# Fused windowed attention and squared-ReLU MLP: dense steps, products, transposes and an overlap copy put in another order

## The chip, the cores and the metric

The kernel runs on one core of a Trainium2 chip. The metric is the device time of one execution in microseconds. The kernel before took 306.08 us, the median of five runs (305.75 to 309.16).

## The reference

Attention over 8 batch rows, 8 heads, 576 positions and 64 values a head, then a two-layer MLP. Heads 0 to 3 see the last 32 positions (sliding), heads 4 to 7 every fourth of the last 128 (dilated).

```python
def _attn_ref(q, k, v):
    B, H, S, D = q.shape                       # 8, 8, 576, 64
    scores = 1.0 / np.sqrt(D) * np.matmul(q, k.transpose(0, 1, 3, 2))
    rel = pos[:, None] - pos[None, :]
    mask_plain = (rel >= 0) & (rel < 32)
    mask_dil = (rel >= 0) & (rel < 128) & (rel % 4 == 0)
    ...
    attn = np.exp(scores - max)
    attn = attn / (np.sum(attn, axis=-1, keepdims=True) + 1e-09)
    return np.matmul(attn, v)

def _moe_ref(x, w_in, w_out):                  # x 4608x512, w_in 512x2048, w_out 2048x512
    h = x @ w_in
    r = np.maximum(h, 0.0)
    return (r * r) @ w_out
```

## The kernel before

**Two kinds of work on TensorE.** A *row* is one of the 8 batch rows of attention (576 tokens). A *dense group* c is 512 of the 4608 tokens in the MLP, so there are 9, numbered 0 to 8. Row b's attention runs interleaved with dense group b − 1. Dense work is written as Python generators in the list `pending`; `pump(n)` (L521) takes n steps of it. So the order of every engine's instructions is written out by hand: attention code issues some matmuls, calls `pump(gap)`, issues the next. `manual_schedule` (L70) keeps that order; each engine executes its own instructions in the order written and waits on semaphores for operands and free buffers. A PSUM tile comes from `papool` (tag pa, 2 buffers, attention) or `pmool` (tag pm, 4 buffers, dense work and some transposes).

**A dense group.** `mm1_gen` (L319) makes 16 tiles ph of 128×512 (L305), with two matmuls a step and four a tile; ScalarE applies ReLU (rt, L328) and VectorE squares it (g, L329). After tiles 11 and 15, `sum_of_g` (L336) makes sums of g, gs[0] and gs[1] (L338, L339). Groups 0 and 1 multiply by w_out plainly (po, L450; group 0 in the order of `mm2_by_rows_gen`). Groups 2 to 8 use `mm2_strassen_gen` (L360): seven products of 256-wide matmuls (L382) into three PSUM banks A, Bk and Ck, shown by the profile as pa, pb and pc. Each product is 2 token tiles × 8 matmuls, and a step ends after four of them. `take` (L396) has ScalarE copy bank A out (ou for the upper half, ov for the lower), `add` (L408) has VectorE add another bank, `leave` (L401) stores on SP's DMA queue. VectorE overwrites gs[1] once in the course of it (L425), since a later product takes other sums.

**A row.** `attn_scores` (L713) makes two groups of sliding scores (ps, L588) and two of dilated ones (pz, L613), each followed by exponentials on ScalarE (L572), masks on VectorE (L575) and a `pump`. `attn_values` (rows 1 to 3) and `attn_values_by_dma` (rows 4 to 7) multiply by v (sliding: pav, L643, three tiles; dilated: paw, L659, four), with a reciprocal and a scaling by VectorE each (L626, L631 into xs and xd), and bring x into xT.

**What a row needs beforehand.** Transposed q and k come from DMA: GpSimd's queue loads ns (sliding) and rewrites the dilated q and k in DRAM as dd; VectorE reorders ns into nr (`by_token`, L120); SP's queue writes nr to DRAM as dp (L224) and transposes dp into QKTp (L232) and dd into QKTd (L236). `turn` (L859) is reorder and dp together. Row 1 alone has its transposes on TensorE (pt L545, pd L562). v is loaded by SP as f32 into sv and sd (L132, L137), and GpSimd casts it into vp and vd (L169, L177). Blocks of v overlap: the last 32 partitions of vp's block m − 1 are needed also as the first 32 of block m, and 64 partitions of vd likewise. Rows 0 to 2 copy the overlap on ScalarE (L184, L189); row 3 and row 4 by SP's DMA (L201, L204); rows 5 to 7 copy that of vp on VectorE (L196) at the end of the dense group and that of vd by DMA (L204).

**Where the loads of rows 3 and 4 stand.** `turn_and_load` (L874) issues on SP: dp, sv, sd, then the transposes QKTp and QKTd, and on GpSimd both casts. For row 3 it is called in row 2's `attn_values` after the third pav; for row 4 as a hook of row 3's `attn_scores` after the last dilated scores. At the top of the next iteration GpSimd waits for the row's transposes (`after_transposes`, L241, a copy into `seen`) and then issues ns and dd of the row after. Rows 5 to 7 already have their transposes ahead of sd and cast vd after the ns and dd issues.

Of the kernel before, what the change touches and what calls it, by code (L numbers as in the profile page):

```python
# [13 lines left out]
P = 128  # L14
# [3 lines left out]
def kernel(  # L18
# [9 lines left out]
    nc = tc.nc  # L28
# [18 lines left out]
    NB = S // QB  # L47
    PADP = P - QB
# [33 lines left out]
    HF = NFF // 2  # L82
    HTOK = TOKC // 2
    wt = [wpool.tile([P, HF, HM], FP16, name=f"wt{n}") for n in range(4)]
    gs = [wpool.tile([P, HF, HTOK], FP16, name=f"gs{n}") for n in range(2)]
# [48 lines left out]
    def load_dilated_v(b, eng):  # L134
        vv = v[b, HH:H].rearrange("h (i c) d -> i h (c d)", c=DIL)
        for t in range(2):
            eng.dma_start(out=sd[P - QD[t] : P, t, :, :], in_=vv[Q0D[t] : Q0D[t] + QD[t]])  # L137
# [54 lines left out]

    at_end: list = []

    def halo_sliding_at_end(b):
        nc.vector.tensor_copy(  # L196
            vp[b % 2][0:PADP, 1:NB, :, 0:D], vp[b % 2][P - PADP : P, 0 : NB - 1, :, 0:D]
        )

    def halo_sliding_by_dma(b):  # L200
        nc.sync.dma_start(out=vp[b % 2][0:PADP, 1:NB], in_=vp[b % 2][P - PADP : P, 0 : NB - 1])  # L201

    def halo_dilated_by_dma(b):
        nc.sync.dma_start(out=vd[b % 2][0:64, 1], in_=vd[b % 2][64:P, 0])  # L204
# [1 line left out]
    def cast_v(b):  # L206
        cast_sliding_v(b)
        cast_dilated_v(b)
# [75 lines left out]
    for r in range(2):  # L284
        nc.vector.tensor_scalar(
            out=vd[r][:, 0, :, :, D],
# [73 lines left out]
    def mm2_strassen_gen(c, g):  # L360
        A, Bk, Ck = "abc"
        banks = {}

        def wq(r, q):
            return lambda k: wo[2 * r + k // 4][:, k % 4, HM * q : HM * (q + 1)]

        def gq(i, r):
            return lambda k, t: g[:, HF * r + k, HTOK * i + P * t : HTOK * i + P * (t + 1)]

        def tq(n):  # L370
            return lambda k: wt[n][:, k]

        def sq(n):
            return lambda k, t: gs[n][:, k, P * t : P * (t + 1)]

        def product(bank, a, b, ts=(0, 1)):
            new = bank not in banks
            if new:
                banks[bank] = pmool.tile([P, 2, HM], FP32, name=f"p{bank}{c}", tag="pm")
            for t in ts:  # L380
                for k in range(HF):
                    nc.tensor.matmul(  # L382
                        banks[bank][:, t],
                        a(k, t),
                        b(k),
                        start=(new and t == 0 and k == 0),
                        stop=(k == HF - 1),
                        skip_group_check=True,
                    )
                    if k % 4 == 3 and (t, k) != (ts[-1], HF - 1):  # L390
                        yield

        def half(i):
            return otp.tile([P, 2, DM], FP32, name=f"o{i}_{c}", tag="ot")

        def take(o, j):  # L396
            ot = o[:, :, HM * j : HM * (j + 1)]
            nc.scalar.copy(ot, banks[A])  # L398
            return ot

        def leave(o, i, js):  # L401
            t0 = c * TOKC + HTOK * i
            m = slice(HM * js[0], HM * (js[-1] + 1))
            nc.sync.dma_start(
                out=out[t0 : t0 + HTOK, m].rearrange("(t p) m -> p t m", p=P), in_=o[:, :, m]
            )

        def add(ot, bank):  # L408
            nc.vector.tensor_add(ot, banks[bank], ot)  # L409

        last = c == NTOKC - 1

        nc.vector.tensor_sub(g[:, 0:HF, HTOK:], g[:, 0:HF, 0:HTOK], g[:, 0:HF, HTOK:])
        yield from product(A, gq(0, 0), wq(0, 0))
        upper = half("u")
        o11 = take(upper, 0)
        yield
        yield from product(Ck, gq(0, 1), wq(1, 0), (0,))
        yield
        yield from product(A, sq(1), tq(1))  # L420
        lower = half("v")
        o21 = take(lower, 0)
        yield
        yield from product(Bk, gq(1, 0), tq(2))
        nc.vector.tensor_sub(gs[1], g[:, HF:, 0:HTOK], gs[1])  # L425
        yield
        yield from product(A, sq(0), tq(0))
        o22 = take(lower, 1)
        add(o22, Bk)
        if last:  # L430
            leave(lower, 1, (1,))
        yield
        yield from product(Ck, gq(0, 1), wq(1, 0), (1,))
        add(o11, Ck)
        if last:
            leave(upper, 0, (0,))
        yield
        yield from product(A, sq(1), wq(1, 1))
        take(upper, 1)
        leave(upper, 0, (1,) if last else (0, 1))  # L440
        while at_end:
            at_end.pop()()
        yield
        yield from product(Bk, gq(1, 1), tq(3))
        add(o21, Bk)
        leave(lower, 1, (0,) if last else (0, 1))
        yield
# [73 lines left out]
    def pump(n):  # L521
        for _ in range(n):
            while pending:
                try:
                    next(pending[0])
                    break
                except StopIteration:
                    pending.pop(0)
# [184 lines left out]
    def attn_scores(b, gap, less=0, hooks={}):  # L713
        for hp in range(2):
            s_sliding(b, hp)
            if hp in hooks:
                hooks[hp]()
            pump(gap)
        for g in range(2):
            s_dilated(b, g)  # L720
            if 2 + g in hooks:
                hooks[2 + g]()
            if g and b < 3:
                halo_sliding(b, 0)
            pump(gap - less)

    def attn_values(b, gap, wide=False, then=None):
        xs = x_tiles(b)
        for mp in range(3):
            av_sliding(b, mp, xs)  # L730
            if b < 3:
                if mp < 2:
                    halo_sliding(b, mp + 1)
                else:
                    halo_dilated(b, 0)
            if then and b == 2 and mp == 2:
                then()
            pump(gap)
        x_sliding(b, 0, xs, wide)
        if b < 3:  # L740
            halo_dilated(b, 2)
        pump(gap)
        av_dilated(b, 0, 0, xs)
        if then and b == 1:
            then()
        pump(gap)
        x_sliding(b, 1, xs, wide)
        pump(gap)
        av_dilated(b, 0, 1, xs)
        pump(gap)  # L750
        for a in range(2):
            av_dilated(b, 1, a, xs)
            pump(gap)
        x_dilated(b, 0, xs, wide)
        pump(gap)
        x_dilated(b, 1, xs, wide)
# [85 lines left out]
    n, m = nsd[1]  # L842
    for hp in range(2):
        t_sliding(1, n, hp, True)
        pump(3)
    for a in range(2):
        t_dilated(1, m, a, True)
        pump(2)
    attn_scores(1, 2, 1)
    dp = []  # L850
    attn_values(1, 1, True, lambda: dp.append(keep_sliding_qk(2, by_token(2, ns))))
    pump(1000)
# [9 lines left out]
    for b in range(2, 4):  # L862
        pending.append(moe_gen(b - 1))
        nxt = b + 1
        after_transposes(b)
        ns = load_sliding_qk(nxt)
        if b == 2:
            cast_v(b)
        dd = keep_dilated_qk(nxt)
        if b == 3:  # L870
            halo_sliding_by_dma(b)
            halo_dilated_by_dma(b)

        def turn_and_load():  # L874
            dp = turn(nxt, ns)
            load_sliding_v(nxt)
            load_dilated_v(nxt, nc.sync)
            transpose_sliding(nxt, dp)
            transpose_dilated(nxt, dd)
            cast_v(nxt)  # L880

        pump(22 if b == 2 else 12)
        attn_scores(b, 4, 0, {3: turn_and_load} if b == 3 else {})
        attn_values(b, b, False, turn_and_load)
        pump(1000)

    for b in range(4, B):
        pending.append(moe_gen(b - 1))
        nxt = b + 1
        if nxt < B:  # L890
            after_transposes(b)
            ns = load_sliding_qk(nxt)
            dd = keep_dilated_qk(nxt)
        if b > 4:
            cast_dilated_v(b)
        else:
            halo_sliding_by_dma(b)
        halo_dilated_by_dma(b)
        dps = []

        def copied():
            if nxt < B:
                dps.append(turn(nxt, ns))

        def first(y):
            if nxt < B:
                load_sliding_v(nxt)

        def second(y):
            if nxt < B:  # L910
                transpose_sliding(nxt, dps[0])
                transpose_dilated(nxt, dd)
                load_dilated_v(nxt, nc.sync)
                nc.gpsimd.tensor_copy(seen, y[:, 0, 0, 0:1])
                cast_sliding_v(nxt)
                at_end.append(lambda: halo_sliding_at_end(nxt))

        pump(3)
        attn_scores(b, 3)
        attn_values_by_dma(b, (copied, first, second))  # L920
        pump(1000)
# [33 lines left out]
```

## Time and profile before

| | |
|---|---|
| median of five runs | 306.08 us |
| the profiled execution's own time | 305.86 us |
| its span in the trace | 304.1 us |
| PE busy | 287.3 us |
| VectorE (DVE) busy | 211.0 us |
| ScalarE (ACT) busy | 173.3 us |
| GpSimd (POOL) busy | 63.3 us |
| DMA packets' time, share of 16 engines, SP's queue / GpSimd's | 51.1% / 26.5% |

The span is the time from the first to the last instruction in the trace; 1.8 us of the execution's own time lie around it. Row 1's transposes and attention lie between 40 and 62 us, row 3's from 100.6 to about 127, rows 4, 5, 6 and 7 begin at 128.4, 158.2, 188.9 and 219. Groups 7 and 8 run alone from 248 us on; PE ends at 300. In a timeline row stand the start, the duration, the engine, the line, out<-in and the count, and at the end in brackets the engine's idle time before it with the releaser. In a row of the table of stretches stand the stretch, its length, the engine's busy time (and count), the granted clock, the DMA share and GB/s. Matmul ends are modelled, so starts are the better measure.

### The profile page before, as it was taken

The page shows a single profiled execution, that of the slowest core. Times are in us where ns is not written, and L with a number is a line of the kernel's source. Part 1 is how long each engine was busy: PE and PEld are TensorE (multiplying, and loading weights), DVE is VectorE, ACT ScalarE, POOL GpSimd, SP SyncE. Part 2 cuts the span into 40 slices and gives each one's busy share as a digit, 9 for nine tenths or more (in the row PEclk, how much of TensorE's full clock was granted, in tenths as well). Part 3 has the DMA queues.
Part 4 walks back from the last instruction along what each step waited for, and adds up shares of the span by engine and source line. Part 5 has one row for each costly group of instructions (what it writes and reads, how often), then busy time and mean ns, then how long its engine had stood idle before and what let it go on. Part 6 is the DMA issues. An engine that isn't in the chain of part 4 may idle for free.

```text
span 304.1 us, 6890 instructions
## 1 busy us (share of the span) xinstructions
PE 287.3 (94%) x2760; PEld 192.6 (63%) x2760; DVE 211.0 (69%) x437; ACT 173.3 (57%) x293; POOL 63.3 (21%) x112
## 2 busy tenths in 40 slices
PE   1888998999999999999999999999999999999994
PEld 1555554455554458755898977557756975785583
DVE  7684548858862798589849994999399834734652
ACT  2765648578835863495359544953496346425620
POOL 4491009001613502320027002700230000000000
PEclk9999999999999999999999999999999999999999
DMA  7899996999689999996799999998983230003004
GB/s 114 192 186 215 207 183 110 178 220 232 127 193 188 249 190 200 229 215 125 132 158 267 192 139 189 267 175 161 173 243 30 49 136 4 2 1 138 2 1 138
DMA packets 77471, 46.77 MB, mean 154 GB/s; under 512 B 58432, under 2 KB 69184, under 8 KB 77440
## 3 DMA queue, kind: packets, MB, share of 16 engines
q1 hardware_dynamic: 68688, 32.71, 51.1%
q0 software_dynamic: 8752, 13.63, 26.5%
q8 instruction: 21, 0.34, 0.5%
q14 instruction: 10, 0.08, 0.1%
HBM read 36.70 MB, written 16.52 MB: 175 GB/s over the span
## 4 chain that ended last, share of the span: by engine, by line
PE 74%; DMA 10%; DVE 9%; POOL 2%; issue 2%; ACT 1%; SPq 0%; DVEq 0%; POOLq 0%
PE ph L305 30%; PE pa L382 15%; PE po L450 8%; PE pb L382 8%; DMA vd<-vd 4%; PE pc L382 3%; DMA nd<-in_q_dram 3%; PE paw L659 2%; DVE g L329 2%; DVE AT L575 2%; DMA QKTp<-dp 2%; DVE xd L631 2%; PE pf L516 2%; DMA QKTd<-dd 1%; PE pav L643 1%
## 5 line engine op out<-in xcount | busy, mean ns | idle before, releaser
L305 PE MATMUL ph<-xT,wi 128*128 128x512 f16 (+1 forms) x640 | 134.2, 359 | 0.7 <-ACT xT L696 0.7
L328 ACT ACTIVATE rt<-ph 128x512 f16<-128x512 f32 x144 | 86.2, 609 | 44.9 <-PE ph L305 42.5
L305 PEld LDWEIGHTS <-wi 128*128 128x128 f16 x640 | 68.2, 114 | 45.8 <-issue 0.6
L329 DVE TENSOR_TENSOR g<-rt 128x512 f16<-128x512 f16 x144 | 62.4, 445 | 37.9 <-ACT rt L328 36.8
L382 PEld LDWEIGHTS <-g 128*128 128x128 f16 x448 | 43.3, 98 | 6.5 <-DVE g L329 0.4
L382 PEld LDWEIGHTS <-gs 128*128 128x128 f16 x336 | 32.0, 98 | 5.4 <-DVE gs L339 1.8
L450 PE MATMUL po<-wo,g 128*128 128x512 f16 x128 | 33.1, 379 | 0.0
L382 PE MATMUL pa<-wt,gs 128*128 128x256 f16 x224 | 27.6, 273 | 1.0 <-DVE gs L339 1.0
L409 DVE TENSOR_TENSOR ov<-pb,ov 128x512 f32<-128x512 f32 x14 | 9.7, 691 | 25.7 <-ACT ov L398 13.0
L382 PE MATMUL pb<-wt,g 128*128 128x256 f16 x224 | 27.1, 273 | 0.0
L398 ACT COPY ov<-pa 128x512 f32<-128x512 f32 x14 | 8.2, 585 | 31.4 <-PE pa L382 31.4
L169 POOL CAST vp<-sv 128x512 f16<-128x512 f32 x24 | 14.8, 646 | 52.4 <-DMA sv<-in_v_dram 41.6
L177 POOL CAST vd<-sd 128x512 f16<-128x512 f32 (+1 forms) x32 | 21.7, 708 | 10.2 <-DMA sd<-in_v_dram 7.9
L631 DVE TENSOR_TENSOR xd<-paw,rcp_d 80x512 f16<-80x512 f32 (+1 forms) x32 | 21.9, 685 | 1.1
L572 ACT ACTIVATE AT<-pz 128x576 f16<-128x576 f32 x32 | 19.8, 695 | 1.2 <-PE pz L613 1.1
L575 DVE TENSOR_TENSOR AT<-AT,maskd 128x576 f16<-128x576 f16 x32 | 18.7, 611 | 1.7 <-ACT AT L572 0.6
L572 ACT ACTIVATE AT<-ps 128x576 f16<-128x576 f32 x32 | 19.2, 658 | 1.3 <-PE ps L588 0.8
L575 DVE TENSOR_TENSOR AT<-AT,maskp 128x576 f16<-128x576 f16 x32 | 15.9, 510 | 4.9 <-ACT AT L572 3.4
L631 DVE TENSOR_TENSOR xs<-pav,rcp_p 96x512 f16<-96x512 f32 x24 | 16.5, 687 | 0.8
L398 ACT COPY ou<-pa 128x512 f32<-128x512 f32 x14 | 8.2, 585 | 13.4 <-PE pa L382 13.4
L450 PEld LDWEIGHTS <-g 128*128 128x128 f16 x128 | 10.4, 97 | 8.3
L659 PEld LDWEIGHTS <-AT 128*128 128x128 f16 x256 | 11.9, 98 | 5.6 <-PE paw L659 1.3
(81 smaller groups left out, 276.3 us busy)
## 6 DMA issues: line engine op xcount, KB each, us to landing
sv<-in_v_dram SPq DMA_DIRECT2D x14, 288.0 KB, 5.2
dp<-nr SPq DMA_DIRECT2D x12, 288.0 KB, 3.9
out_dram<-ou SPq DMA_DIRECT2D x6, 512.0 KB, 4.2
out_dram<-ov SPq DMA_DIRECT2D x6, 512.0 KB, 4.4
sd<-in_v_dram SPq DMA_DIRECT2D x8, 320.0 KB, 5.7
ns<-in_k_dram POOLq DMA_DIRECT2D x8, 288.0 KB, 6.8
ns<-in_q_dram POOLq DMA_DIRECT2D x8, 288.0 KB, 8.0
sd<-in_v_dram SPq DMA_DIRECT2D x8, 256.0 KB, 5.2
```

The source lines that it names most:

```text
L169: nc.gpsimd.tensor_copy(vp[b % 2][:, m : m + 2, :, 0:D], sv[:, :, m : m + 2, :].rearrange("p h m d -> p m h d"))
L177: nc.gpsimd.tensor_copy(vd[b % 2][p0:P, t, c : c + 2, :, 0:D], sd[p0:P, t, :, D * c : D * (c + 2)].rearrange("p h (c d) -> p c h d", d=D),)
L305: nc.tensor.matmul(ph[:, t0:t1], wi4[ffc // 4][:, dmk, :, ffc % 4], xT[:, dmk, x0 : x0 + t1 - t0], start=(dmk == 0 and t0 == 0), stop=(dmk ...
L328: nc.scalar.activation(rt, ph[:], ACTF.Relu)
L329: nc.vector.tensor_mul(g[:, ffc, :], rt, rt)
L382: nc.tensor.matmul(banks[bank][:, t], a(k, t), b(k), start=(new and t == 0 and k == 0), stop=(k == HF - 1), skip_group_check=True,)
L398: nc.scalar.copy(ot, banks[A])
L450: nc.tensor.matmul(po, g[:, ffc, t * P : (t + 1) * P], wo[ffc // 4][:, ffc % 4, :], start=(ffc == 0), stop=(ffc == NFF - 1),)
L572: nc.scalar.activation(AT[:, u, 0:UW], ps[:, :, 0 : UW // 2], ACTF.Exp, scale=scale)
L575: nc.vector.tensor_mul(AT[:, u, 0:UW], AT[:, u, 0:UW], mask)
L631: nc.vector.tensor_tensor(out=x, in0=pv, in1=rb, op=ALU.mult)
L659: nc.tensor.matmul(pav[:, e, h * (D + 2) : h * (D + 2) + D + 1], AT[:, 4 + h, off : off + P], vd[b % 2][:, t, 2 * a + e, h, 0 : D + 1], st ...
```

## The change

- `mm2_strassen_gen` (all groups from 2 on): the product of Ck runs whole after the first product of A, with the add of o11 right behind it, where it had stood in two halves. The second half of Bk's product takes the place of the second half of Ck's. The gs[1] subtraction stands after `take` instead of behind Bk's product.
- Row 1: `pump(3)` after each sliding transpose becomes 2, that after the second dilated transpose 1; the pumps after the two dilated score groups become 2 instead of 1, the one after pav 0 becomes 2. The sum stays 17 steps.
- Rows 3 and 4: transposes go ahead of sd on SP's queue. For row 4 the whole of it (nr, dp, sv, transposes, sd) moves from the hook after row 3's last scores to after row 3's second pav. GpSimd casts only vp there; vd is cast after the ns and dd issues of the next iteration. The overlap of vp is copied by VectorE: for row 3 as a hook after the second sliding scores, for row 4 at the end of dense group 2; the two DMAs go.
- Row 3's first pump is 9 steps instead of 12, so three more dense steps stand behind the scores.

On the engines, built: SP loses two vp DMAs, ScalarE's and PE's instruction counts stay, VectorE has two copies more. On SP the last stores of the closing group change places (the first half of u ahead of the second half of v).

```diff
-    def halo_sliding_at_end(b):
+    def halo_sliding_at_once(b):
         nc.vector.tensor_copy(
             vp[b % 2][0:PADP, 1:NB, :, 0:D], vp[b % 2][P - PADP : P, 0 : NB - 1, :, 0:D]
         )
-
-    def halo_sliding_by_dma(b):
-        nc.sync.dma_start(out=vp[b % 2][0:PADP, 1:NB], in_=vp[b % 2][P - PADP : P, 0 : NB - 1])
@@ mm2_strassen_gen
-        yield from product(Ck, gq(0, 1), wq(1, 0), (0,))
+        yield from product(Ck, gq(0, 1), wq(1, 0))
+        add(o11, Ck)
+        if last:
+            leave(upper, 0, (0,))
         yield
         yield from product(A, sq(1), tq(1))
         lower = half("v")
         o21 = take(lower, 0)
+        nc.vector.tensor_sub(gs[1], g[:, HF:, 0:HTOK], gs[1])
         yield
-        yield from product(Bk, gq(1, 0), tq(2))
-        nc.vector.tensor_sub(gs[1], g[:, HF:, 0:HTOK], gs[1])
+        yield from product(Bk, gq(1, 0), tq(2), (0,))
         yield
         yield from product(A, sq(0), tq(0))
         o22 = take(lower, 1)
+        yield
+        yield from product(Bk, gq(1, 0), tq(2), (1,))
         add(o22, Bk)
         if last:
             leave(lower, 1, (1,))
-        yield
-        yield from product(Ck, gq(0, 1), wq(1, 0), (1,))
-        add(o11, Ck)
-        if last:
-            leave(upper, 0, (0,))
         yield
         yield from product(A, sq(1), wq(1, 1))
@@ attn_values
-            if then and b == 2 and mp == 2:
+            if then and b > 1 and mp == 4 - b:
                 then()
-            pump(gap)
+            pump(gap + (b == 1 and mp == 0))
@@ row 1
         t_sliding(1, n, hp, True)
-        pump(3)
+        pump(2)
     for a in range(2):
         t_dilated(1, m, a, True)
-        pump(2)
-    attn_scores(1, 2, 1)
+        pump(2 - a)
+    attn_scores(1, 2)
@@ rows 2 and 3
         if b == 3:
-            halo_sliding_by_dma(b)
+            cast_dilated_v(b)
             halo_dilated_by_dma(b)
 
         def turn_and_load():
             dp = turn(nxt, ns)
             load_sliding_v(nxt)
-            load_dilated_v(nxt, nc.sync)
             transpose_sliding(nxt, dp)
             transpose_dilated(nxt, dd)
-            cast_v(nxt)
-
-        pump(22 if b == 2 else 12)
-        attn_scores(b, 4, 0, {3: turn_and_load} if b == 3 else {})
+            load_dilated_v(nxt, nc.sync)
+            cast_sliding_v(nxt)
+            if nxt > 3:
+                at_end.append(lambda: halo_sliding_at_once(nxt))
+
+        pump(22 if b == 2 else 9)
+        attn_scores(b, 4, 0, {1: lambda: halo_sliding_at_once(b)} if b == 3 else {})
         attn_values(b, b, False, turn_and_load)
@@ rows 4 to 7
-        if b > 4:
-            cast_dilated_v(b)
-        else:
-            halo_sliding_by_dma(b)
+        cast_dilated_v(b)
         halo_dilated_by_dma(b)
```

More of the change, by code (lines that the diff above doesn't have):

```diff
@@ L915, in second @@
                 cast_sliding_v(nxt)
-                at_end.append(lambda: halo_sliding_at_end(nxt))
+                at_end.append(lambda: halo_sliding_at_once(nxt))
         pump(3)
```

## The prediction

> **What bounds the kernel now.** I read the page first (shares, slices, groups), then the table of stretches, then PE's waits, then PE's timeline wherever one of its rows carries an idle time, and last VectorE's timeline in those places.
>
> ```profile
> span 304.1 us, 6890 instructions
> ...
> PE 287.3 (94%) x2760; PEld 192.6 (63%) x2760; DVE 211.0 (69%) x437; ACT 173.3 (57%) x293; POOL 63.3 (21%) x112
> ...
> PEclk9999999999999999999999999999999999999999
> ```
>
> PE is the bound and runs at the full clock, so only time in which PE stands still can be won; nothing here removes a matmul. From 25 us to 300 us PE is almost always busy. Its stalls are small, and I size each by the start of the late matmul against the start that was due (undisturbed, a 512-wide matmul follows the last after 216 ns, a 256-wide one after 109 ns). The bracket at a row's end gives the idle time and its releaser:
>
> ```profile
> 50.73 0.31 PE L613 MATMUL pz<-QKTd 64*128 64x80 f16 x8 [0.23 <-ACT AT L572]
> ...
> 52.24 0.29 PE L643 MATMUL pav<-vp,AT 128*128 128x65 f16 x4 [0.54 <-ACT vp L184]
> ...
> 54.23 0.41 PE L643 MATMUL pav<-vp,AT 128*128 128x65 f16 x8 [0.58 <-DVE rcp_p L626]
> ```
> ```profile
> 100.63 0.43 PE L588 MATMUL ps<-QKTp 64*128 64x96 f16 x12 [0.31 <-DMA QKTp<-dp]
> ...
> 112.98 0.41 PE L643 MATMUL pav<-vp,AT 128*128 128x65 f16 x8 [0.32 <-DVE xs L631]
> ```
> ```profile
> 177.21 0.60 PE L382 MATMUL pa<-wt,gs 128*128 128x256 f16 x4
> 178.28 1.48 PE L382 MATMUL pa<-wt,gs 128*128 128x256 f16 x12 [0.48 <-DVE gs L339]
> ```
>
> Row 1 loses 0.24+0.42 at the dilated scores, 0.71 at pav 0 and 0.74 at pav 2, and 0.5 in three short waits behind it: 2.6 us. Row 3 loses 0.48 before its scores, 0.48 at its third pav and 0.17 at 115.85: 1.13 us. In row 5, four matmuls from 177.21 make the fifth due at 177.65; it starts at 178.28, so 0.63 is lost. Row 6 repeats it (207.76 + 0.44 = 208.20 due, 208.84 started): 0.64. Rows 4 and 7 lose nothing there. That is 5.0 us in all that the edits could reach; the first 25 us and the last 4 us are not touched.
>
> The second thing to see is what GpSimd's casts do to VectorE. These windows are VectorE's busy time:
>
> ```profile
> 163.50:166.50 3.00, 3.00 (x5) 1.00 1.12 280
> ...
> 130.30:133.30 3.00, 2.55 (x7) 1.00 1.02 172
> ```
>
> Row 5 has the four vd casts (L177) in this window, row 4 has none: VectorE does 5 instructions where it otherwise does 7. A mask that takes 0.46 us took 0.86 to 0.98, a square of 0.42 took 0.83. Summed, the four casts cost VectorE 1.9 us in row 5, 1.7 in row 6, 1.5 in row 7.
>
> **Strassen's order (all dense groups from 2 on).** The product Ck = gq(0,1)·wq(1,0), 16 matmuls, is now issued whole ahead of the product with gs[1]; before, 8 came there and 8 later. The count stays. PE therefore has 8 × 109 ns = 0.87 us more to do before it needs gs[1]. In rows 5 and 6 the fifth gs matmul becomes due at 177.65 + 0.87 = 178.52 and at 209.07, while gs is ready at 178.23 and 208.78: both stalls go, with 0.29 to spare. Gain 0.63 + 0.64 = **1.27 us**. What can be late next is the other gs[1] subtraction (L425, 1.21 us), since the add of o11 (0.69) now stands before it on VectorE. In row 5 it ended at 182.16; plus 0.69 is 182.85; it is needed at 183.97 − 0.63 = 183.34. Margin 0.5, so nothing is lost. ACT's copy out of bank A (0.59) now has one 0.87 us block of another product to hide in, as it had before around Ck. In the two closing dense groups PE had no stall and keeps none; the store of the v half leaves about 0.9 us later, still ahead of the last one, which follows the last product as before: 0, at most +0.2.
>
> **Row 1.** Seventeen dense steps (two 512-wide matmuls, 0.43 each) stand among row 1's transposes, scores and first pav in both; three move from the transposes to behind the two dilated score groups and pav 0. So the scores start earlier. Replayed with the trace's own durations: the second transposes wait 0.1 for the copy ending 41.14; the first scores then wait for VectorE's QKTd copy (0.82, ends about 45.2) and start near 45.3 instead of 46.35, a new stall of 0.4. The exponentials, each 0.65 on ACT, follow 1.07 earlier. pz group 1 and pav 0 then wait some 0.15 and 0.5. VectorE reaches the xs of pav 0 at about 53.0 instead of 54.08, and pav 2 starts near 53.3 instead of 54.23, with as many dense steps behind it as before: 0.9 gained. Part goes back: the nr copy waits for ns, whose loading GpSimd issues at 48.3 behind a DMA and not behind PE (landed 56.7), and the last paw wait for VectorE behind it. I take **−0.6**, ends −0.9 and −0.2.
>
> **Row 3.** Three dense steps move behind the scores: they are due at 100.63 − 0.48 (the stall) − 3 × 0.43 = 98.9. Do their transposed operands come by then? On SP's queue the order was:
>
> ```profile
> 85.03 1.13 SPq L224 DMA_DIRECT2D dp<-nr  x2
> 86.26 3.30 SPq L132 DMA_DIRECT2D sv<-in_v_dram  x2
> 89.65 3.51 SPq L137 DMA_DIRECT2D sd<-in_v_dram  x2
> 93.25 4.89 SPq L232 DMA_TRANSPOSE QKTp<-dp  x2
> ```
>
> The two sd issues (3.51 us of queue, 576 KB) now follow the transposes. The first dp landed at 90.97, so the QKTp transposes issue from about 91.0 and land near 97 to 98.5 (5.6 from issue to landing in this window; 100.59 was the last landing before). The 0.48 stall goes. The price lies behind it: sd lands near 103 instead of 98, GpSimd casts vd only after the ns and dd loads of row 4 (two each, 2.4 us), so from about 103.2 to 105.9, in the middle of the scores, where VectorE has 1.76 us of work (two squares, two masks) in each 2.2 us step. Before, they ran from 97.98 to 100.71 and cost 0.6. VectorE also gets the sliding overlap of v (L196's shape, 0.485 in rows 5 to 7) in place of SP's DMA of 2.6 us, and loses nothing for it; nr (0.75) moves behind pav 1. Replayed: the masks of pz group 1 end near 108.7, two squares and the gs sums (2 × 0.42 and 2 × 0.69) near 111.0, the reciprocal and xs of pav 0 near 111.9, so the third pav, due 11.8 after the first scores as before, at 110.7, starts near 112.05: a stall of 1.35 where the old ones of this row were 1.13. **+0.2**. With the casts wholly in VectorE's gaps the stall is 0.7 (−0.5 for the row); with all of 1.7 on the path it is about 2.1 (+1.0). The dilated overlap by DMA (2.7) then leaves near 105 and lands by 110; paw 1 needs it near 121.
>
> A rule of the Trainium skill weighs here: the page "SBUF — State Buffer", section "SBUF: two separate sides", calls the port pair of VectorE and GpSimd an exclusive lock held for a whole instruction, the loser blocking fully. By that, four VectorE instructions would each wait out a cast of up to 0.69: 2.8 us a row. The row shows 1.5 to 1.9, so I use 1.7. By the rule row 3 would stall 1.1 more and row 4 0.85 (its second gs sum 1.8 later, 0.97 covered), and the sum below would be 306.4.
>
> **Row 4.** nr goes about 3 us later in row 3 (near 114.6), sd leaves the way, so QKTp of row 4 should land by about 126, near the old 126.25, before its scores at 128.4: 0. Its vd casts move, too, from 121.8–124.2, where they cost VectorE nothing, into its scores, as in rows 5 to 7. There the second gs sum came 0.9 later after the scores than in row 4; the Ck block covers 0.87 and row 4 had about 0.1 in hand. **0**, at most +0.6. The vp copy for row 4 waits at the group's end for GpSimd's cast, behind it only an add with slack: 0.
>
> **Sum.** −1.27 − 0.6 + 0.2 + 0 = −1.67. The profiled execution took 305.86 (span 304.1 and 1.8 around it) and becomes 304.2; the median, 306.08, stands 0.2 above it: **304.4 us**.
>
> **The rivals.**
> Row 3 pays nothing: transposes early and the casts in VectorE's gaps. Then row 3's three stalls go, 1.13, and row 1 gives 0.9: −3.3, so 302.8. For it: VectorE idles 0.2 to 0.4 between squares near 105. Against: the gs sums stand before the xs in either order.
> VectorE becomes the bound in rows 3 and 4, the end on the other side. Place: the xs of row 3's pav 0 and row 4's second gs sum. Price, for a cast cost of c a row: c − 1.48 in row 3 (1.35 − 1.13 at 1.7), c − 1.97 in row 4; against −1.87 from rows 1, 5 and 6 it decides from c = 2.66 on. At the rule's 2.8 the sum is +0.3: 306.4. For it: VectorE is full from 108.5 to 119. Against: no row of the trace paid over 1.9.
> The transposes don't come sooner: the DMA share in this stretch is about 1, and moved bytes are not fewer. Then QKTp lands at 100.6, the scores wait 1.7 where the sum has none: +1.3 after rounding down for VectorE, which catches up meanwhile, so 305.7. Against: SP's queue, not the engines' share, held them from 91.0 to 93.25.
>
> **How the numbers follow.** Forecast 0.5, free row 3 0.17, VectorE bound 0.15, late transposes 0.18. About 1% (3 us) is what a measurement of this kernel surely tells from no change. Faster by over 1% (under 303.0) is the free case and a little of the forecast: 0.19; slower by over 1% (over 309.1) is only the far end of the VectorE case: 0.06; the rest, 0.75, within 1%. The range reaches from the free case, 302.7, a little past the VectorE case, to 306.6; the forecast's own is 303.4 to 305.3.
>
> **What would show it.** No idle time at the gs matmuls (L382 before, a few lines up now) of rows 5 and 6; row 1's pav 2 near 53.3; row 3's first scores near 98.9 (less what row 1 gained) without a DMA wait and its third pav waiting 1 to 1.5 us for xs; masks or squares of 0.83 us in rows 3 and 4 beside the vd casts. A wait of row 4's scores for QKTp, or of its gs product, would prove me wrong, and so would a row 1 whose new wait at the first scores is as long as the one it removes.

## The result, and the profile after

| | before | after |
|---|---|---|
| median over all runs | 306.34 us (52 runs) | 305.22 us (31 runs) |
| ratio, 95% interval | | 0.997 (0.9956 to 0.9984) |
| the profiled execution's own time | 305.86 us | 306.36 us |

The ratio is that of the fast executions, without those over 1.5% above the fastest of their kernel. The changed kernel is 0.92 us faster (0.49 to 1.35, the interval times 306.34): inside the range and within 1%, but a little over half of the 1.67 us that the sum gave. Its profiled execution took 1.1 us more than its median, that of before 0.5 less than its own, so the two spans say nothing of a change of 1 us. The page after, first lines:

```profile
span 304.3 us, 6887 instructions
...
PE 287.0 (94%) x2760; PEld 192.9 (63%) x2760; DVE 214.3 (70%) x439; ACT 173.2 (57%) x293; POOL 65.5 (22%) x112
...
PEclk9999999999999999999999999999999999999999
```

PE is busy as long as before, at the same clock. So only its standing still can differ. I therefore compare by stages, from the first matmul of one dense group to that of the next (group b − 1 runs beside row b), and over all profiles whose code is the same in the stage. The 21.1 to 22.9 us ahead of group 0, where nothing was edited, show what one profile alone can mislead by.

| stage | forecast | old code, mean (profiles) | new code, mean (profiles) | difference |
|---|---|---|---|---|
| row 1 | −0.6 | 39.76 (8) | 39.70 (7) | −0.05 |
| row 2 | 0 | 32.81 (all) | 32.81 (all) | 0 |
| row 3 | +0.2 | 32.19 (4) | 31.73 (10) | −0.46 |
| row 4 | 0 | 29.78 (all) | 29.78 (all) | 0 |
| rows 5 to 7 | −1.27 | 91.31 (4) | 90.83 (6) | −0.48 |
| groups 7, 8 and the end | 0 to +0.2 | 56.31 (8) | 56.43 (12) | +0.13 |
| sum | −1.67 | | | −0.86 |

The sum of the stages agrees with the timed −0.92. From the scatter of the profiles, the standard errors of the differences are 0.19 us in row 1, 0.29 in row 3 and 0.26 in rows 5 to 7, so a single row's difference is known to some tenths only. (Profiles of the experiments below are counted with the code that they have in that stage; row 3's stage holds dense group 2, so old means the old order of products too. Four profiles with the new order and row 3 as before have a mean of 31.90. Row 2 leaves p_row1's 33.32 out and row 1 its 44.93; that profile has its own section at the end.)

Row 1's stage begins with group 0, where nothing was edited, and that took 15.91 us in two profiles of the old code and 16.49 in all others. From the first po matmul on, row 1 took 23.41 us with the old code and 23.21 with the new: −0.20.

PE's timeline, after, row 5's products and row 6's scores:

```profile
177.37 1.04 PE L379 MATMUL pc<-wo,g 128*128 128x256 f16 x8
178.24 1.91 PE L379 MATMUL pa<-wt,gs 128*128 128x256 f16 x16
...
186.97 1.46 PE L302 MATMUL ph<-xT,wi 128*128 128x512 f16 x6
188.79 0.43 PE L585 MATMUL ps<-QKTp 64*128 64x96 f16 x12 [0.36 <-DMA QKTp<-dp]
```

The product with gs has no bracket any more: the stall is gone as forecast. But the scores, due 1.39 us after the first of six dense matmuls (row 7 before, shown below, which waits for nothing), so at 188.36, start at 188.79. A new wait of 0.43 has come behind the old one. PE's waits, after, group them (sum and count, then the longest):

```profile
PE ps L585 <- DMA QKTp<-dp: 1.5, 3, 0.7
```

Row 7 shows it best. SP's queue and PE, before:

```profile
211.60 1.20 SPq L708 DMA_TRANSPOSE yd<-xd  x1
212.90 2.73 SPq L232 DMA_TRANSPOSE QKTp<-dp  x2
```
```profile
218.02 1.46 PE L305 MATMUL ph<-xT,wi 128*128 128x512 f16 x6
219.41 0.43 PE L588 MATMUL ps<-QKTp 64*128 64x96 f16 x12
```

and after:

```profile
211.74 1.19 SPq L705 DMA_TRANSPOSE yd<-xd  x1
213.03 2.73 SPq L229 DMA_TRANSPOSE QKTp<-dp  x2
```
```profile
217.50 1.46 PE L302 MATMUL ph<-xT,wi 128*128 128x512 f16 x6
219.40 0.43 PE L585 MATMUL ps<-QKTp 64*128 64x96 f16 x12 [0.44 <-DMA QKTp<-dp]
```

PE comes to these six matmuls 0.52 us sooner, and the scores start at the same time: due at 218.89, they wait 0.51. The transposes are issued no sooner, since they stand on SP's queue behind the second yd, and that hangs on VectorE's last xd, ahead of the products in which the stall was won.

In row 1 the new order works as replayed in its first part, and in this profile the gain ends at the last paw. PE, after:

```profile
44.95 0.43 PE L585 MATMUL ps<-QKTp 64*128 64x96 f16 x12 [0.39 <-ACT QKTd L163]
...
51.09 0.29 PE L640 MATMUL pav<-vp,AT 128*128 128x65 f16 x4 [0.36 <-ACT vp L184]
...
58.44 0.42 PE L656 MATMUL paw<-vd,AT 128*128 128x65 f16 x8 [0.80 <-DVE rcp_d L623]
```

and VectorE, after:

```profile
55.28 0.69 DVE L628 TENSOR_TENSOR xd<-paw,rcp_d 80x512 f16<-80x512 f32 x1
56.70 0.76 DVE L120 COPY nr<-ns 128x2304 f16<-128x2304 f16 x1 [0.73 <-DMA ns<-in_q_dram]
```

The nr copy, for row 2, stands idle until ns has landed, and the reciprocal of row 1's next paw is held behind it; PE waits for that. But only two of the seven profiles of the new code have this wait (n_nocast is the other). The rest is lost ahead of pav 2. GpSimd casts row 1's v from about 45 to 52 us, once sv has landed, and the masks, now earlier, fall into that time. The last four casts and the masks of the dilated scores, after:

```profile
49.39 3.01 POOL L177 CAST vd<-sd 128x512 f16<-128x512 f32 x4
...
48.77 3.16 DVE L572 TENSOR_TENSOR AT<-AT,maskd 128x576 f16<-128x576 f16 x4
```

and in n_before, the old code again:

```profile
48.10 3.02 POOL L177 CAST vd<-sd 128x512 f16<-128x512 f32 x4
...
50.56 2.01 DVE L575 TENSOR_TENSOR AT<-AT,maskd 128x576 f16<-128x576 f16 x4
```

Beside a cast a mask takes about 0.86 us, otherwise 0.45. All eight masks of row 1 sum to 6.11 to 6.88 us in the seven profiles of the new code, mean 6.42, and to 5.18 to 6.48 in the eight of the old, mean 5.81. With the old code pav 2 follows that sum: where it is under 5.4, pav 2 waits 0.15, where it is over 5.9, 0.29 to 0.84. Counted from the first po matmul, pav 2 starts at 15.47 us in the mean of the old code and at 15.07 with the new: 0.40 is won there, and the wait for ns takes 0.20 of it back in the mean.

In row 3 the scores and the third pav, after:

```profile
98.56 0.43 PE L585 MATMUL ps<-QKTp 64*128 64x96 f16 x12
...
111.19 0.42 PE L640 MATMUL pav<-vp,AT 128*128 128x65 f16 x8 [0.61 <-DVE xs L628]
```

The scores start 0.2 late at most (QKTp landed at 98.5, in two other profiles of this kernel at 97.0 and 96.3), so the transposes did come sooner; of all ten profiles with this row 3, only r_after has its scores wait for QKTp (0.55). The third pav waits 0.77 against a forecast of 1.35. VectorE's busy time beside the vd casts, in row 3 and in row 4:

```profile
104.90:107.90 3.00, 2.97 (x5) 1.00 1.13 242
...
130.80:133.80 3.00, 2.95 (x4) 1.00 1.12 305
```

Four or five instructions where seven fit: the casts make VectorE slow here as they did in row 5. Summed over the instructions beside them they cost it 1.5 us in row 3 and 1.65 in row 4.

### The profile page after: what moved, and what is told of

Its sections match the earlier page's. It is cut to its first block, busy times and chain, and to the rows that moved or that the text cites. A ratio compares the mean times of both kernels' runs of the same rounds, so it can differ in the third digit from the quotient of the medians.

```text
span 304.3 us, 6887 instructions
## 1 busy us (share of the span) xinstructions
PE 287.0 (94%) x2760; PEld 192.9 (63%) x2760; DVE 214.3 (70%) x439; ACT 173.2 (57%) x293; POOL 65.5 (22%) x112
## 4 chain that ended last, share of the span: by engine, by line
PE 71%; DMA 19%; DVE 5%; POOL 2%; issue 1%; ACT 1%; SPq 0%; POOLq 0%
PE ph L302 34%; PE pa L379 14%; DMA sv<-in_v_dram 7%; PE pb L379 6%; DMA QKTp<-dp 5%; PE po L447 5%; DMA wi<-in_moe_w_in_dram 5%; PE pc L379 4%; DMA ns<-in_q_dram 3%; PE paw L656 2%; PE ps L585 2%; PE pav L640 1%; PE pz L610 1%; DVE g L326 1%; POOL vp L169 1%
## 5 line engine op out<-in xcount | busy, mean ns | idle before, releaser
L379 PE MATMUL pb<-wt,g 128*128 128x256 f16 x224 | 27.9, 273 | 0.0
L169 POOL CAST vp<-sv 128x512 f16<-128x512 f32 x24 | 15.6, 684 | 52.6 <-DMA sv<-in_v_dram 37.5
L177 POOL CAST vd<-sd 128x512 f16<-128x512 f32 (+1 forms) x32 | 22.9, 741 | 12.2 <-PE pz L610 8.9
L572 DVE TENSOR_TENSOR AT<-AT,maskd 128x576 f16<-128x576 f16 x32 | 20.6, 672 | 1.0 <-ACT AT L569 0.5
```

The costliest lines, as they stand in the source:

```text
L169: nc.gpsimd.tensor_copy(vp[b % 2][:, m : m + 2, :, 0:D], sv[:, :, m : m + 2, :].rearrange("p h m d -> p m h d"))
L177: nc.gpsimd.tensor_copy(vd[b % 2][p0:P, t, c : c + 2, :, 0:D], sd[p0:P, t, :, D * c : D * (c + 2)].rearrange("p h (c d) -> p c h d", d=D),)
L379: nc.tensor.matmul(banks[bank][:, t], a(k, t), b(k), start=(new and t == 0 and k == 0), stop=(k == HF - 1), skip_group_check=True,)
L572: nc.vector.tensor_mul(AT[:, u, 0:UW], AT[:, u, 0:UW], mask)
```

## The experiments

All ratios are against the kernel before on the same chip. The stages are those of the table above.

| run | ratio, 95% interval | row 1 | row 3 | rows 5 to 7 |
|---|---|---|---|---|
| p_strassen | 0.9979 (0.9957 to 1.0001) | 39.95 | 32.19 | 90.77 |
| p_row1 | 0.9980 (0.9957 to 1.0004) | 44.93 | 31.63 | 91.20 |
| p_rows34 | 1.0001 (0.9983 to 1.0019) | 40.27 | 32.50 | 91.78 |
| p_after | 0.9948 (0.9924 to 0.9973) | 39.55 | 31.92 | 91.07 |
| q_qktp | 0.9985 (0.9964 to 1.0006) | 39.44 | 31.87 | 91.39 |
| q_ns | 0.9948 (0.9929 to 0.9966) | 39.27 | 31.60 | 90.46 |
| q_both | 0.9971 (0.9952 to 0.9989) | 39.27 | 31.39 | 92.53 |
| s_qktp | 1.0015 (0.9989 to 1.0042) | 39.60 | 31.52 | 90.87 |
| r_strassen | 1.0035 (1.0014 to 1.0055) | 39.70 | 32.36 | 91.19 |
| r_before | 1.0023 (1.0004 to 1.0042) | 39.74 | 32.96 | 91.37 |
| r_after | 1.0014 (0.9994 to 1.0034) | 39.25 | 32.17 | 91.70 |
| r_both | 1.0005 (0.9986 to 1.0025) | 39.26 | 31.73 | 91.80 |
| h_strassen | 0.9970 (0.9949 to 0.9992) | 39.01 | 31.52 | 89.84 |
| h_after | 0.9940 (0.9920 to 0.9961) | 39.65 | 31.59 | 90.13 |
| h_both | 0.9941 (0.9919 to 0.9963) | 39.76 | 31.75 | 90.30 |
| h_again | 0.9963 (0.9941 to 0.9984) | 39.79 | 31.39 | 90.52 |

The last two experiments, n_nocast and n_before, are single executions. The theory: each stall won hands PE on to the next operand that is late, the row's QKTp in rows 5 to 7 and ns in row 1. The rival: VectorE, with the casts moved into the scores, takes the gain back.

**One part alone.** p_strassen, p_row1 and p_rows34 are the kernel before with only the Strassen order, only row 1's pumps, or only what is changed for rows 3 and 4; p_after is the whole change again.

> The kernel before with the new order of Strassen's products alone. Theory A (given back at the next row's scores): the 0.64 us stalls at the gs matmuls of rows 5 and 6 go, but the scores of rows 6 and 7, now due 0.6 us earlier, wait for the DMA that fills QKTp, so the time falls by 0 to 0.6 us (305.7 to 306.3 against 306.3). Rival (the gain holds): no wait at the scores, 1.27 us less, 305.0.

> The kernel before with row 1's dense steps alone moved. Theory B (row 1 becomes bound by the loading of ns for row 2): the nr copy waits for ns, which lands near 56.7 us whatever PE does, and the first matmul of dense group 1 comes 0 to 0.5 us earlier than in the kernel before: 305.8 to 306.3. Rival (the gain of the prediction): 0.6 to 0.9 us less, nr not waiting.

> The kernel before with rows 3 and 4 alone changed (transposes ahead of dilated v, overlap of v on VectorE, three dense steps behind row 3's scores). The profile of the changed kernel says about -0.2 us from the scores of row 3 to the first matmul of group 3 and 0 in row 4: 306.1. The prediction's step says +0.2: 306.5. With VectorE held up by the casts at the rule's price: +1 or more. Against Strassen's old order row 4's gs matmul has only 0.1 us in hand, so a stall of 0.5 to 0.9 us there, as in rows 5 and 6, would show what the moved casts cost: then 306.6 to 307.0.

> The changed kernel again, for a second profile. If the waits of the scores of rows 5 to 7 for QKTp (0.90, 0.52 and 0.60 us in the first profile) belong to the order of work, they are there again, 0.4 us or more each; if they were a slow moment of that execution, they are under 0.2 us. Time 305.2.

By the ratios the differences are −0.64, −0.61 and +0.03 us, together −1.2, and −1.6 for the whole, none of the parts sure by itself. The traces tell more. In p_strassen, which has no cast moved, row 7's scores wait 0.77 for QKTp and rows 5 to 7 take 90.77, the mean of the new code: the rival is not needed for the gain lost there. In p_after, row 7's wait is there again (0.60), but not row 5's, and row 6's is 0.14; so only row 7's belongs to every execution. In p_rows34, with the old order of products, row 3 has a stall that the whole change does not have (PE's timeline):

```profile
114.81 0.60 PE L379 MATMUL pa<-wt,gs 128*128 128x256 f16 x4
116.04 0.61 PE L379 MATMUL pa<-wt,gs 128*128 128x256 f16 x4 [0.62 <-DVE gs L336]
```

So the edits of row 3, the casts among them, make gs 0.79 late on PE, against 0.17 in the kernel before, and the whole block of Ck covers it: the parts are not independent, and the sum had priced row 3 without this.

**QKTp ahead of the second yd, and ns sooner.** q_qktp moves both transposes of QKTp behind the sv issue; q_ns issues row 2's ns loads on GpSimd ahead of row 1's vp casts; q_both has both. s_qktp is q_qktp's edit on the kernel before with the Strassen order.

```diff
         def first(y):
             if nxt < B:
                 load_sliding_v(nxt)
+                transpose_sliding(nxt, dps[0])
         def second(y):
             if nxt < B:
-                transpose_sliding(nxt, dps[0])
...
     load_v(1)
+    ns = load_sliding_qk(2)
     cast_sliding_v(1)
     load_w_out((3,))
-    ns = load_sliding_qk(2)
```

> The changed kernel with the transposes into QKTp for rows 5 to 7 issued on SP right behind the loads of sv, ahead of the transpose of the second yd. Theory A (the freed time of PE is spent waiting for QKTp): the operands land some 2 us earlier, no matmul of the scores of rows 5 to 7 waits (0.2 to 0.9 us each in two profiles of the changed kernel), and the stage from group 4 to group 7 shortens by 0.7 to 1.6 us: time 303.8 to 304.6. Rival (QKTp is only a symptom of busy DMA engines): they wait for QKTp or QKTd all the same, 305.3.

> The changed kernel with the loads of ns for row 2 issued on GpSimd's queue ahead of row 1's casts of vp, so several us earlier. Theory B (row 1 is bound by ns): nr never waits for ns, the stage from group 0 to group 1 takes 39.3 to 39.6 us in the profile (40.2 and 39.6 in two profiles of the changed kernel), time 0 to 0.7 us less than the changed kernel: 304.6 to 305.2. Rival: the earlier loads delay sv of row 1 on the DMA engines as much, and nothing is won: 305.3 or more.

> Both of these in the changed kernel. If the two waits are what gave the gain back, the parts add: 303.2 to 304.4, faster than both kernels. If only one was real, it equals the better of the two single runs.

> The kernel before with Strassen's new order and the earlier QKTp transposes, rows 1, 3 and 4 as before. Theory A: now the whole 1.27 us of the prediction's step shows: from group 4 to group 7 89.7 us instead of 91.0 in the profile of the kernel before, no wait for gs and none for QKTp, 304.9 to 305.4 against 306.5 to 306.9. Rival (PE's gain goes elsewhere): 306 or more.

In q_ns nr has no idle time ahead of it (VectorE's timeline), and row 1 takes 39.27. It does not test ns alone, though: the edit also takes the ns issues out of GpSimd's way, so that the casts of dilated v come earlier and the masks of the dilated scores take 0.55 us in the mean, against 0.84 in the new code. In time q_ns stands at 0.9948, where p_after stood without the edit.

```profile
56.55 0.75 DVE L120 COPY nr<-ns 128x2304 f16<-128x2304 f16 x1
```

q_qktp takes QKTp's waits away and puts a longer one elsewhere. SP's queue and PE, row 6:

```profile
179.72 3.71 SPq L229 DMA_TRANSPOSE QKTp<-dp  x2
183.48 1.28 SPq L705 DMA_TRANSPOSE yd<-xd  x1
```
```profile
186.17 0.81 PE L302 MATMUL ph<-xT,wi 128*128 128x512 f16 x3
188.71 0.81 PE L302 MATMUL ph<-xT,wi 128*128 128x512 f16 x3 [1.74 <-ACT xT L693]
```

Two transposes hold the queue 3.71 us, and the second yd, whose last xd was ready at 180.18, leaves 3.3 late. Dense group 5's matmuls (the next expectation says 6) wait 1.9 for the xT that is made of it. s_qktp waits 1.4 in the same place, q_both 1.2 there and 1.85 in group 6.

**QKTp ahead of both yd.** The r kernels issue the two transposes between xT's and the first yd: r_before on the kernel before, r_strassen with the Strassen order, r_after on the changed kernel, r_both with q_ns's edit too.

```diff
         x_sliding_by_dma(b, xs)
+        then[3]()
         ys = []
...
+        def between():
+            if nxt < B:
+                transpose_sliding(nxt, dps[0])
...
-                transpose_sliding(nxt, dps[0])
...
-        attn_values_by_dma(b, (copied, first, second))
+        attn_values_by_dma(b, (copied, first, second, between))
```

> The kernel before with Strassen's new order, and the transposes into QKTp of rows 5 to 7 issued on SP between the transposes of xs and of the first yd, so that neither yd waits behind them. The last attempt (behind sv) made the second yd 2.6 us later and dense group 6 waited 1.4 to 1.9 us for it. Theory A: with both out of the way the 1.27 us of the two gs stalls appear in full, from group 4 to group 7 89.5 to 89.8 us (91.0 in the kernel before), no wait for QKTp. Rival: some other wait takes it, 90.5 or more.

> The kernel before with those earlier QKTp transposes alone. Theory A: PE gains nothing in the mean execution beyond the rare wait, since in its old order the scores were due just after the operands landed: stage from group 4 to group 7 90.7 to 91.0, both gs stalls of 0.64 still there. Rival (the QKTp chain alone is what bounds rows 5 to 7): 90.0 or less.

> The changed kernel with those earlier QKTp transposes. Theory A: the waits of 0.2 to 0.9 us ahead of the scores of rows 5 to 7 go, stage from group 4 to group 7 89.5 to 89.9 us (91.67 and 91.07 in two profiles of the changed kernel), time about 304.2, 1 to 1.5 us less than the changed kernel. Rival: 305.2, as the changed kernel.

> That, and the earlier loads of ns for row 2, which alone gave 304.6: if both waits are what held the change back, 303.2 to 303.8, under both kernels by about 1%; from group 0 to group 1 39.3 us and from group 4 to group 7 89.5 to 89.9.

All four lose what they win: rows 5 to 7 take 91.19 to 91.80, and the ratios of r_strassen and r_before are clear of 1 on the slow side. ScalarE and PE, r_after, row 5:

```profile
182.41 1.26 ACT L693 COPY xT<-yd 128x640 f16<-128x640 f16 x1 [2.56 <-DMA yd<-xd]
183.58 0.58 ACT L395 COPY ov<-pa 128x512 f32<-128x512 f32 x1
```
```profile
184.21 1.91 PE L379 MATMUL pa<-wo,gs 128*128 128x256 f16 x16 [1.49 <-ACT ov L395]
```

Now the first yd is late, ScalarE stands 2.56 us at the xT copy, and the copy out of bank A is behind it in order; PE waits 1.65 for the bank.

**One transpose into the queue's own pause.** Before the second yd SP's queue stands idle about 1.5 us (210.11 to 211.60 in row 7, before), nearly room for one transpose. The h kernels put one there and leave the other: h_strassen on the kernel before with the Strassen order, h_after on the changed kernel, h_both with q_ns's edit too; h_again is the changed kernel.

```diff
         def first(y):
             if nxt < B:
                 load_sliding_v(nxt)
+                transpose_sliding(nxt, dps[0], (1,))
         def second(y):
             if nxt < B:
-                transpose_sliding(nxt, dps[0])
+                transpose_sliding(nxt, dps[0], (0,))
```

> The kernel before with Strassen's new order, and one of the two transposes into QKTp of rows 5 to 7 issued ahead of that of the second yd, while SP waits for it anyway. Theory A: QKTp lands about 1.3 us earlier, yd no later; from group 4 to group 7 89.6 to 90.2 us (91.0 in the kernel before, 90.8 with Strassen's order alone). Rival (no time to be had on SP's queue): 90.7 or more, with a wait for yd or QKTp.

> The changed kernel with that one transpose moved. Theory A: from group 4 to group 7 89.6 to 90.2 us (91.67 and 91.07 in two profiles of the changed kernel), time 0.5 to 1.3 us under the changed kernel of the same chip. Rival: the same time within 0.3 us.

> That and the earlier ns of row 2: the two savings add, 0.8 to 1.8 us under the changed kernel of the same chip, 303.3 to 304.4, and under the kernel before by 0.6 to 0.9%.

> The changed kernel itself: 0.3 to 0.5% under the kernel before, and a third profile, with waits of rows 5 to 7's scores for QKTp that sum to 0.5 us or more.

SP's queue and PE, h_strassen, row 7:

```profile
208.58 2.39 SPq L232 DMA_TRANSPOSE QKTp<-dp  x1
211.02 1.27 SPq L708 DMA_TRANSPOSE yd<-xd  x1
212.34 1.37 SPq L232 DMA_TRANSPOSE QKTp<-dp  x1
```
```profile
217.49 0.43 PE L588 MATMUL ps<-QKTp 64*128 64x96 f16 x12
```

No wait is left at these scores. But the transpose takes longer than the pause, and the second yd leaves behind it: its last xd was ready at 210.31, 0.7 us sooner. In row 6 of h_strassen it is worse, with the xd ready at 179.98:

```profile
179.32 2.56 SPq L232 DMA_TRANSPOSE QKTp<-dp  x1
181.93 1.27 SPq L708 DMA_TRANSPOSE yd<-xd  x1
```

There PE waits 0.28 for the xT made of that yd, in h_after 0.48 and in h_both 0.54. Rows 5 to 7 take 89.84, 90.13 and 90.30 in the three kernels, mean 90.09: 1.22 (standard error 0.22) under the old code's 91.31, where the forecast had 1.27. So nearly the whole Strassen gain is there once its next obstacle is out of the way; that the two figures agree so closely is scatter, since the waits for xT are still in it. The times show it less well. h_after and h_both stand at 0.994 and h_again, on the same chip, at 0.9963, and the intervals overlap; the medians lie 0.39 and 0.69 us under h_again's, where 0.5 to 1.3 and 0.8 to 1.8 were expected. h_both has the lowest median of that chip, 304.03 us against 306.03 before and 304.72 for the changed kernel. The ns edit is the less sure of the two: the four profiles with ns early have a mean row 1 of 39.39, 0.31 (standard error 0.18) under the seven with it late, but in the pairs from one chip row 1 took 39.27 against 39.44 (q_both, q_qktp), 39.26 against 39.25 (r_both, r_after) and 39.76 against 39.65 (h_both, h_after).

**The casts themselves.** n_nocast is the changed kernel without the casts of dilated v in rows 3 and 4; n_before is the kernel before.

```diff
         if b == 3:
-            cast_dilated_v(b)
             halo_dilated_by_dma(b)
...
-        cast_dilated_v(b)
+        if b > 4:
+            cast_dilated_v(b)
```

> The changed kernel without GpSimd's casts of dilated v for rows 3 and 4 (those rows then use the dilated v of rows 1 and 2, so the output is not the reference's there). If the casts make row 3's third pav wait, that wait falls from 0.4 to 0.9 us to 0.3 or less and no mask or square of these scores takes more than 0.5 us; the prediction said 1.35 with and 0.7 without. If the gs sums and the overlap copy do it, the wait stays above 0.4. Row 4's stage stays 29.8 either way.

> The kernel before again. Its stages from group 4 to group 7 sum to 90.9 to 91.8 us, with the two gs stalls of 0.64, and from group 0 to group 1 it takes 39.7 to 40.3.

Row 3's third pav and VectorE's busy time, n_nocast:

```profile
110.29 0.42 PE L640 MATMUL pav<-vp,AT 128*128 128x65 f16 x8
```
```profile
104.20:107.20 3.00, 2.49 (x6) 1.00 1.16 187
```

The stall falls to 0.19. With the casts it is 0.77, 0.90 and 0.37 in three profiles of the changed kernel, and 0.65 in the mean of all ten with this row 3. So the casts put 0.2 to 0.7 us of their 1.5 on PE. Row 3 takes 31.21 without them, 31.73 on average with them. Row 4 is 29.77 without and 29.78 with: there they cost PE nothing. The single times, 304.24 us beside 308.38 and, for n_before, 306.27, carry no verdict.

## Why the prediction was right in part

- **What bounds it: right.** PE's matmuls were as many and as fast; everything turned on stalls of a few tenths.
- **Strassen, −1.27 forecast, −0.48 found.** Both stalls went, as worked out. The step that failed is "What can be late next is the other gs[1] subtraction": that was not late, and I had not looked beyond the products. Late next was QKTp at the following row's scores. The trace of before had the number: its last landing was 1.35, 0.63 and 0.2 us ahead of the scores of rows 5, 6 and 7. Row 5's stall of 0.63 was just covered in row 6, row 6's 0.64 met 0.2 in row 7. That alone leaves 1.27 − 0.44 = 0.83. In the six profiles with the new order, row 7's scores wait 0.41 to 0.77, and all waits for QKTp have a mean of 0.79 us, against 0.23 with the old order (one of four profiles, p_rows34, waits 0.91 in row 7). Another 0.15 is lost in the mean at the pav of rows 5 and 6, where PE waits for VectorE's xs (0.31 to 0.35, in three of the six). Row 5's 0.8 in the first profile after is a late landing: issued at 151.1, QKTp took 7.2 us to the last landing, against 5.2 before.
- **Row 1, −0.6 forecast, −0.05 found, or −0.20 without group 0's part.** The mis-sized term is the 0.9 at pav 2: 0.40 was found there. One half of what is missing was never to be won: pav 2's wait, 0.74 in the one trace read, has a mean of 0.46 in the eight profiles of the old code (0.15 to 0.84). The other half comes from the replay "with the trace's own durations": the earlier masks run longer beside GpSimd's casts, and pav 2 still waits 0.24 in the mean. What ns takes back was named ("Part goes back") and about right: 0.3 in the sum, and in the runs 0.8 and 0.6 in two of seven profiles and nothing in five. That the casts hold pav 2 back rests on the durations in these traces; no run moved row 1's casts alone.
- **Row 3, +0.2 forecast, −0.46 found.** Transposes near 97 to 98.5 and scores at 98.6: right. The mis-sized term is the third pav's stall, 1.35 in the sum and 0.37 to 0.90 in the runs. The casts' price on VectorE was right (1.4 to 2.0 us a row for 1.7), but less than half of it came to PE; and without them the stall was 0.19, not the 0.7 that the replay gave. Also the 0.48 that row 3's scores lost before was 0.38: a score follows a dense matmul after 0.31 us undisturbed, not after 0.216. By the exclusive lock's 2.8 a row, the rule weighed in the prediction, the stall would have been 2.45; the price read from the trace was the better one.
- **Row 4: right,** 29.78 in every kernel with all of its parts.
- **The end, 0 to +0.2 forecast, +0.13 found,** in every kernel that has rows 3 and 4 changed, with the old product order too (30.38 after group 8's first matmul in p_rows34, against 30.27). So it is not the late store of the v half, as the sum had it. The extra lies behind the last landing, 2.96 us after PE's end in both. What causes it stays open.
- **The rivals.** VectorE as the bound of rows 3 and 4 needs 2.66 us a row and got 2.0 at most; what the casts cost VectorE did take a smaller part elsewhere, in row 1. The transposes were late in row 3 in one profile of ten. The free row 3 is near what single profiles show (0.37 at its third pav in two).

That the total still is over half of the forecast is in part luck: row 3 came out 0.66 better than its term, and with that term as forecast the stages would sum to −0.2.

## What to carry to other kernels

A removed stall is worth at most the slack of the next operand that does not depend on it: before counting it, read from the trace how long each later operand had landed before its use, and find where its chain branches off. On a DMA queue that issues in the order written, moving a transfer forward makes those behind it late; only what fits the queue's own pause would be free, and here even one transpose overran it by 0.6 to 2.0 us. A replay with one trace's durations misses that an instruction moved beside another engine's casts takes longer. Where landings differ between executions, compare by stages over several profiles, and don't price a stall from one.

## What the runs showed of the hardware

One profile of p_row1 took 310.39 us where its median is 306.14. There ns landed at 58.50 and VectorE's nr waited 2.80 us, and PE behind it. PE's stretches of that profile (length, busy time and count, granted clock, DMA share, GB/s):

```profile
56.34:59.75 3.41, 1.13 (x13) 1.00 0.87 156
59.75:63.16 3.41, 2.90 (x23) 0.50 0.72 183
63.16:66.58 3.42, 3.42 (x16) 0.50 1.06 231
66.58:69.99 3.41, 3.41 (x17) 1.00 1.12 214
```

After 2.95 us of standing still PE ran at half clock until 66.58: row 1 took 44.93 us for about 39.8, of which some 2.6 are the wait and the rest the clock, and row 2 took another 0.5 more (33.32 for 32.81). Such a clock gate is what the Trainium skill describes in "TensorE: Matmul & The Clock Gate", section "Part 1: The HAM clock gate (the "warmup" mystery)". It has the clock fall after at least one idle window of about 3.4 us; here a window in which PE was busy for 1.13 us was enough.

The traces say more closely when it falls. In all twenty, a stretch of one clock between two changes is a whole multiple of 3.413 us: the long stretches at full clock, 286.72, 290.13 and 293.55 us, are 84, 85 and 86 of them, and p_row1's 47.79, 6.83 and 242.35 are 14, 2 and 71. So the clock changes only on a grid of that step, wherever the work stands in it. In every step at full clock with 1.14 us or less of matmuls (p_row1's, and the ones after the last matmuls of ten other profiles) the clock fell at its end, and in every step with 1.44 us or more it stayed. A stall near 3 us thus costs clock or not by where it falls on the grid. This one did, and about as much again as its own length.
